# A four-layer kernel with the work of its attention half-steps timed anew and its matrix splits in uneven portions

## The chip, the cores and the metric

The kernel runs on one core of a Trainium2 chip. The metric is the device time of one execution in microseconds (us); with several executions, their median. Everything is float32 on the outside. TensorE (PE) multiplies, VectorE (DVE), ScalarE (ACT) and GpSimd (POOL) do the elementwise work, and nearly all transfers are issued by SyncE (SP) on one queue.

## The reference

The input x has 2048 rows of 640 numbers. Four residual layers follow each other: attention, Fourier mixing, attention, Fourier mixing. Each first normalizes its input by row.

```python
def _A_ref(x, wqkv, wo):
    H = 32; Dh = D // H
    W, dil = 8, 2
    qkv = (lambda x, *d: x.transpose(*d))((x @ wqkv).reshape(B, S, 3, H, Dh), 2, 0, 3, 1, 4)
...
    logits = jnp.einsum("bhsd,bhswd->bhsw", q, kg) * scale
...
    o = jnp.einsum("bhsw,bhswd->bhsd", attn, vg)
    return (lambda x, *d: x.transpose(*d))(o, 0, 2, 1, 3).reshape(B, S, D) @ wo

def _B_ref(x, dft_seq_re, dft_seq_im, dft_hid_re, dft_hid_im):
    a = jnp.einsum("bsd,ed->bse", x, dft_hid_re)
    b = jnp.einsum("bsd,ed->bse", x, dft_hid_im)
    y = jnp.einsum("ts,bse->bte", dft_seq_re, a) - jnp.einsum("ts,bse->bte", dft_seq_im, b)
    return y
```

Attention is local: each row looks at eight rows (itself and every second one before it), in 32 heads of 20 numbers.

## The kernel before

Every float32 factor is split into a high part that TensorE takes in one pass (a cast on ACT) and a low part, the rest (a subtraction on DVE or POOL). A product is then three matmuls: high times high, high times low, low times high (`PASSES`, L283). The rows are held in four chunks c of four tiles j, 128 rows each.

**An attention layer** (`layer_a`) is called twice: for layer 0 (called A0 below, `CFG['ly'][0]`) and for layer 2 (A2, `CFG['ly'][1]`). Its attention runs over 32 units u, eight to a chunk, a unit being four heads, and each unit has two halves jp, so that there are 64 steps, with some 7 steps of entry before them and a few behind them. In a step:

- DVE multiplies the queries with the keys of the window (`qk_mul`, L498); POOL adds the two halves of every product (L501); DVE sums the rest into logits (`qk_red`, L511). A pair (u, jp) listed in `whole` leaves out POOL's addition, and DVE sums twice as many numbers.
- DVE and ACT do the softmax (`soft`, L524 to L537, parts 0 to 5; `soft_exp`, L519). DVE multiplies the weights with the values (`av_mul`, L541), and POOL adds the eight products in three halvings (`av_tree`, L556 to L558).
- ACT copies a unit's queries into PSUM ahead of its first half (`q_copy`, L471).
- TensorE works beside it: `qkv_mm` (L429) makes queries, keys and values, 64 groups g of 15 matmuls, whose results ACT copies out (`qkv_evac`, L436) and SP stores to HBM, from where the windows are loaded; transposes of normalized input or of attention output (`pc_pe`, L394; high part `pc_hi`, L398; the high part subtracted in PSUM, `pc_sub`, L402; low part `pc_lo`, L417); the output projection `wo_mm` (L581), which DVE adds to the residual (`wo_add`, L217); and, in the last 18 steps, the first sequence product of the Fourier layer that follows (`z_mm`, L969), 16 slices of 15 matmuls.
- For that product the new rows are normalized: `ln_hi` on ACT, and the low part `ln_lo` (L919), which `lnv` sends to DVE (1) or POOL (0), one entry for each tile. The reciprocal root of the variance is a power on POOL (`finish`, L239), or, where `lno` of the chunk is true, a logarithm and an exponential on ACT (`var_eps`, L227). The product's other factor, a slice of the cosine matrix, is split in A0 (`c_hi` L941, `c_lo` L954) and read back from HBM already split in A2 (`c_get`, tile c0b).

The order of all this is written by hand. Each piece of work is put at a step and a phase (`at`), and in each step the phases are gone through in the order of the string `ph` (the first for steps below 48, the second for the others); the result is the order of each engine's queue, SP's too. The engines work their queues in order, and between them only data and free buffers make one wait. `gs` gives the step of each QKV group, `wo` those of the projection halves, `z` three times the step of each third of a slice (the remainder picks the phase z0, z1 or pe3), `ln` the step of the normalization, `t2` and `t3` those of the last transposes, `ym` and `ymph` the step and phase of the previous layer's last two output tiles (`ymm`, L1043), `early` the order in which A2's first tiles are transposed inside the end of the layer before, and `wqg` which weight splits of the start go to POOL.

**A Fourier layer** (`LayerB`) is a sequence product by a seven-product scheme (`pair`, L1132), three pairs of row blocks, with the second sequence product and the preparation ahead of it (`run`): cell sums of the matrix blocks (`x_whole` L1088, `x_combine` L1096 to L1098) and the splits of the hidden matrices (`load_w`, L188 to L192) are 38 items that the lists `pre` and `post` deal out over 16 slices of that product. There the order is by hand only for TensorE; a planner orders the rest.

## Time and profile before

| | us |
|---|---|
| three runs: median (lowest to highest) | 1796.12 (1793.09 to 1797.68) |
| the profiled execution, its own time | 1798.85 |
| its span, first to last instruction | 1797.1 |
| TensorE busy | 1737.8 |
| VectorE busy | 1375.7 |
| ScalarE busy | 818.1 |
| GpSimd busy | 633.3 |

How to read it: the profile comes from one execution, and its span is 1.75 us shorter than that execution's own time. GpSimd works only in the two attention layers. A matmul that waits inside a chain of matmuls still counts as busy in part, so the busy time of TensorE is an upper bound of its work. The chain of waits follows the end back from releaser to releaser; the views by stage (windows) give each engine's busy time in a stretch, and the clock granted to TensorE as a share of the full one.

### The profile page before, as it was taken

Reading aid. Unit: us, or ns where it says so; the run is one execution under the profiler, and the core shown is the slowest. Engines: PE = TensorE matmul, PEld = TensorE weight load, DVE = VectorE, ACT = ScalarE, POOL = GpSimd, SP = SyncE. Lnnn points to the kernel's source line nnn. Section 1 sums busy time; section 2 is a strip of 40 time slices with the busy share of each in tenths; the row PEclk is TensorE's granted clock in tenths of the full one; section 3 lists DMA queues with packets and bytes.
Section 4 is the critical chain, followed back from the end, with each engine's and each line's share of the span. In section 5 each row is a group of like instructions: output and inputs, shape, how many; then the busy total and the mean of one; then the engine's idle time right before and its main releaser. Section 6 shows DMA issues by size and latency. Waiting matters only on the chain.

```text
span 1797.1 us, 26504 instructions
## 1 busy us (share of the span) xinstructions
PE 1737.8 (97%) x8798; PEld 1508.5 (84%) x8798; DVE 1375.7 (77%) x2136; ACT 818.1 (46%) x1708; POOL 633.3 (35%) x591
## 2 busy tenths in 40 slices
PE   9999998989999999999999999999899999999999
PEld 6889897778788888888888899987788888888888
DVE  5899889888767767768739988888777676676673
ACT  5554544544445545445533334444434443443441
POOL 3799898960000000000008987889400000000000
PEclk9999998999999999999999999999999999999999
DMA  6786667647787887888747856687687876877861
GB/s 231 225 279 212 202 207 253 221 154 276 255 268 245 292 272 242 291 271 267 246 126 224 283 182 202 202 293 263 218 289 269 258 235 216 272 234 224 264 212 52
DMA packets 273994, 423.59 MB, mean 236 GB/s; under 512 B 22688, under 2 KB 153248, under 8 KB 273600
## 3 DMA queue, kind: packets, MB, share of 16 engines
q1 hardware_dynamic: 270656, 419.92, 71.7%
q10 hardware_dynamic: 3200, 1.97, 0.4%
q8 instruction: 70, 1.15, 0.3%
q14 instruction: 68, 0.56, 0.1%
HBM read 336.66 MB, written 85.14 MB: 235 GB/s over the span
## 4 chain that ended last, share of the span: by engine, by line
PE 67%; DVE 11%; DMA 9%; POOL 7%; ACT 3%; issue 2%; SPq 0%; ACTq 0%; DVEq 0%; POOLq 0%
PE m L429 18%; PE aux L1043 12%; PE t L1132 9%; PE m L1132 9%; PE pq L1132 5%; PE xt L1132 5%; PE aux L581 4%; DMA win<-cs_in 3%; DMA xc<-stg 2%; POOL pr L556 2%; DVE pr L498 2%; POOL pr L501 2%; DVE pr L541 2%; POOL r L919 1%; PE t L969 1%
## 5 line engine op out<-in xcount | busy, mean ns | idle before, releaser
L429 PE MATMUL m<-r,s 128*128 128x480 f32 x1920 | 438.4, 383 | 4.3 <-ACT s L297 3.2
L429 PEld LDWEIGHTS m<-r,s 128*128 128x128 f32 x1920 | 358.0, 189 | 58.6 <-ACT s L297 4.9
L1125 ACT CAST r<-win 128x512 fp32r<-128x512 f32 x251 | 153.0, 620 | 175.3 <-DVE win L1161 90.2
L239 POOL TENSOR_TENSOR stats<-stats,mhalf 128x1 f32<-128x1 f32 (+1 forms) x40 | 28.9, 723 | 567.8 <-ACT stats L233 567.8
L1043 PE MATMUL aux<-r2a,zo 128*128 128x320 f32 x768 | 226.0, 309 | 0.0
L556 POOL TENSOR_TENSOR pr<-pr 128x640 f32<-128x640 f32 x126 | 204.2, 1621 | 36.6 <-DVE pr L541 36.0
L498 DVE TENSOR_TENSOR pr<-pq,win 128x1280 f32<-128x1280 f32 x128 | 189.7, 1483 | 28.7 <-ACT pq L471 26.3
L1043 PE MATMUL aux<-pr,zo 128*128 128x320 f32 x704 | 207.8, 309 | 0.0
L1126 DVE TENSOR_TENSOR r<-win,r 128x512 fp32r<-128x512 f32 x251 | 169.4, 687 | 44.0 <-ACT r L1125 42.1
L541 DVE TENSOR_TENSOR pr<-pq,win 128x1280 f32<-128x1280 f32 x128 | 190.9, 1491 | 4.3
L501 POOL TENSOR_TENSOR pr<-pr 128x640 f32<-128x640 f32 x128 | 183.5, 1434 | 22.0 <-DVE pr L498 19.1
L1132 PE MATMUL m<-r,r 128*128 128x512 f32 x594 | 152.4, 391 | 1.2 <-ACT stg L1097 0.5
L1043 PEld LDWEIGHTS aux<-r2a,zo 128*128 128x128 f32 x768 | 144.2, 188 | 1.9
L969 PE MATMUL m<-s,r 128*128 128x512 f32 x384 | 120.8, 402 | 17.7 <-DMA s<-c0b 8.0
L1043 PEld LDWEIGHTS aux<-pr,zo 128*128 128x128 f32 x704 | 132.2, 188 | 2.0
L1132 PEld LDWEIGHTS m<-r,r 128*128 128x128 f32 x594 | 111.0, 188 | 26.0 <-DVE r L1126 1.4
L1132 PE MATMUL t<-r,r 128*128 128x512 f32 x495 | 132.5, 390 | 0.0
L436 ACT COPY stg<-m 128x480 f32<-128x480 f32 x128 | 71.1, 556 | 115.9 <-PE m L429 100.8
L969 PE MATMUL t<-s,r 128*128 128x512 f32 x384 | 118.0, 396 | 2.4 <-DVE ot L1025 2.4
L511 DVE TENSOR_REDUCE lg<-pr 128x64 f32<-128x640 f32 x128 | 104.2, 814 | 18.0 <-POOL pr L501 17.8
L557 POOL TENSOR_TENSOR pr<-pr 128x320 f32<-128x320 f32 x126 | 114.0, 905 | 9.9
L1132 PEld LDWEIGHTS t<-r,r 128*128 128x128 f32 x495 | 92.9, 188 | 19.9
(271 smaller groups left out, 3221.0 us busy)
## 6 DMA issues: line engine op xcount, KB each, us to landing
win<-cs_in SPq DMA_DIRECT2D x358, 256.0 KB, 4.4
r<-xc SPq DMA_DIRECT2D x240, 256.0 KB, 4.5
win<-kvb SPq DMA_DIRECT2D x96, 440.0 KB, 4.5
xa<-cs_in SPq DMA_DIRECT2D x124, 256.0 KB, 4.3
win<-kvb SPq DMA_DIRECT2D x64, 360.0 KB, 5.0
xc<-stg SPq DMA_DIRECT2D x40, 512.0 KB, 4.8
kvb<-stg SPq DMA_DIRECT2D x60, 320.0 KB, 4.0
xr<-xs SPq DMA_DIRECT2D x40, 320.0 KB, 3.3
```

Source lines behind the costliest of these rows:

```text
L429: nc.tensor.matmul(mt[g][:, : 3 * F], st[:, a, k], wq[q][:, b, k], start=n == 0, stop=n == 14)
L498: nc.vector.tensor_tensor(pr, q, wview(u, jp, 0, [[1, FE]]), op=ALU.mult)
L501: nc.gpsimd.tensor_tensor(pv[:, :, 0:10], pv[:, :, 0:10], pv[:, :, 10:20], op=ALU.add)
L511: nc.vector.tensor_reduce(rows(lgs[u], jp), pv.rearrange("p (a h) d -> p a h d", h=HE), axis=AX.X, op=ALU.add,)
L541: nc.vector.tensor_tensor(pr.rearrange("p j w (h d) -> p (j w) h d", d=DH), rows(lgs[u], jp).unsqueeze(3).to_broadcast([P, 2 * W, HE, DH]) ...
L556: g.tensor_tensor(pr[:, :, 0:4], pr[:, :, 0:4], pr[:, :, 4:8], op=ALU.add)
L557: g.tensor_tensor(pr[:, :, 0:2], pr[:, :, 0:2], pr[:, :, 2:4], op=ALU.add)
L969: self.last = nc.tensor.matmul(self.z[t][k], self.xn[c][:, a, j, k * P : (k + 1) * P], self.ct[s][:, b], start=s == 0 and i == 0, stop=s = ...
L1043: self.last = nc.tensor.matmul(self.ym[e][:, :320], zt[(k, a, ri)][:, j2 * P : (j2 + 1) * P], w[:, e * 320 : (e + 1) * 320], start=(k, a, ...
L1125: nc.scalar.copy(hi, raw)
L1126: nc.vector.tensor_tensor(lo, raw, hi.bitcast(F32), op=ALU.subtract)
L1132: nc.tensor.matmul(bank, w(a, kb), hl[b], start=start and (a, b) == (0, 0), stop=stop and (a, b) == (1, 0),)
```

## The change

The lists of `CFG` are set anew for both attention layers and for the two `run` stages. In A0 two halves, (u, jp) = (16, 1) and (28, 1), become `whole`; the low parts of tiles (0,0), (0,2), (0,3) and (1,1) go from POOL to DVE and those of (3,2) and (3,3) from DVE to POOL; the DVE order puts softmax part 4 ahead of `qk_red` in steps below 48 and `av_mul` ahead of part 1 in the others. In A2 the low part of (0,3) goes to DVE and that of (3,2) to POOL, the statistics of chunks 2 and 3 take the logarithm on ACT, the previous layer's two output tiles stand behind QKV groups 2 and 5 and no longer behind 3 and 4, and the transposes of chunk 2 and 3 that shared steps are spread over more steps. Some QKV groups, projection halves, thirds of slices and loads move by a step or two in both. The items of `run` are dealt out unevenly, a few ahead of a slice.

In `pair` the loading and splitting of an iteration is put into three helpers, so that it could be issued ahead; with `ahead` at [0, 0, 0] and `views` empty nothing is. The splits of an iteration now stand ahead of its products in the program's text (all three in the first loop, the first two in the others), in the same order among themselves as before. The diff, with the second and third helper and the loops that call them cut:

```diff
-CFG = {'nwin': 5,
+CFG = {'views': [],
+ 'ahead': [0, 0, 0],
+ 'nwin': 5,
  'bufs': {'xa': 2, 'qs': 1, 'stg': 2, 'xr': 1},
  'pad2': 16,
  'ot': ['ot'],
- 'wqg': [0, 0, 0, 0, 0, 0, 1, 0, 1, 0, 0, 1, 0, 1, 0, 0, 1, 0, 1, 0],
- 'run': [{'pre': [0, 0, 0, 0, 0, 0, 0, 0, 0, 0, 0, 0, 0, 0, 0, 0],
-          'post': [0, 4, 4, 4, 3, 3, 3, 3, 3, 3, 3, 3, 3, 3, 3, 3],
+ 'wqg': [0, 0, 0, 0, 0, 0, 0, 0, 1, 0, 0, 1, 0, 0, 0, 0, 1, 1, 0, 0],
+ 'run': [{'pre': [0, 0, 0, 0, 0, 0, 0, 1, 0, 0, 0, 4, 0, 0, 0, 0],
+          'post': [1, 5, 4, 2, 3, 3, 2, 6, 3, 1, 0, 3, 1, 3, 3, 3],
           'y': [[6, 6, 6, 6, 6], [13, 13, 16, 16, 16]]},
-         {'pre': [0, 0, 0, 0, 0, 0, 0, 0, 0, 0, 0, 0, 0, 0, 0, 0],
-          'post': [0, 4, 4, 4, 3, 3, 3, 3, 3, 3, 3, 3, 3, 3, 3, 3],
-          'y': [[6, 6, 6, 6, 6], [13, 13, 16, 16, 16]]}],
- 'ly': [{'gs': [-7, -6, -5, -4, -3, -2, -1, 0, 1, 1, 2, 3, 3, 4, 5, 5, 6, 7, 8, 8, 9, 11, 12, 12, 13, 14, 14, 15, 16,
-                16, 17, 18, 18, 19, 20, 21, 22, 23, 24, 25, 26, 27, 28, 29, 30, 30, 31, 32, 33, 34, 34, 35, 36, 37,
-                38, 39, 40, 41, 42, 43, 44, 45, 46, 47],
+         {'pre': [0, 0, 0, 0, 0, 6, 0, 0, 2, 0, 0, 0, 0, 0, 0, 0],
+          'post': [0, 4, 4, 5, 0, 2, 1, 1, 0, 5, 6, 0, 5, 1, 6, 0],
+          'y': [[6, 6, 6, 6, 6], [12, 13, 16, 16, 16]]}],
+ 'ly': [{'gs': [-7, -6, -5, -4, -3, -2, -1, 0, 1, 2, 2, 2, 3, 4, 5, 5, 6, 7, 8, 8, 9, 11, 12, 12, 13, 14, 14, 14, 16,
+                16, 16, 18, 18, 19, 20, 21, 22, 23, 24, 25, 25, 27, 28, 29, 30, 30, 31, 32, 33, 33, 34, 35, 36, 37,
+                39, 39, 41, 41, 42, 43, 44, 45, 46, 46],
          'tx': [4, 6, 8, 10, 16, 18, 20, 22, 30, 32, 34, 36],
-         'ord': [[0, 2, 1, 3, 4, 6, 5, 7], [0, 2, 1, 3, 4, 6, 5, 7], [0, 2, 1, 3, 4, 6, 5, 7]],
+         'ord': [[2, 0, 1, 3, 4, 6, 5, 7], [0, 2, 1, 3, 4, 6, 5, 7], [0, 2, 1, 3, 4, 6, 5, 7]],
          'out': [20, 24, 28, 32, 36, 40, 44, 46],
-         'wo': [22, 23, 26, 27, 30, 31, 34, 35, 38, 39, 42, 43, 46, 47, 48, 49],
+         'wo': [23, 23, 26, 27, 30, 30, 34, 35, 37, 38, 42, 43, 46, 47, 49, 49],
          'woph': 'pe2',
-         'ln': [40, 42, 44, 46, 52, 53, 54, 55],
+         'ln': [40, 43, 44, 46, 53, 53, 55, 54],
          'w2': [52, 53, 54, 55],
          'w3': [60, 61],
          'lnown': [4, 3],
-         'z': [149, 149, 149, 152, 152, 152, 155, 156, 157, 161, 161, 164, 170, 170, 170, 173, 173, 173, 173, 173,
-               173, 174, 176, 176, 179, 179, 179, 179, 180, 181, 185, 188, 188, 188, 191, 191, 191, 191, 194, 195,
-               199, 200],
+         'z': [149, 149, 151, 151, 151, 152, 152, 154, 155, 161, 163, 163, 170, 170, 170, 172, 173, 173, 174, 175,
+               176, 176, 177, 178, 180, 182, 182, 182, 185, 185, 185, 186, 186, 188, 191, 191, 191, 191, 194, 195,
+               198, 200],
          'early': [3, 3, 6.5, 8.7, 5, 6, 7, 8.5, 10, 11, 14, 14.1, 8],
          'ym': [-3, -2],
          'ymph': 'pe3',
-         't2': [48, 48, 48, 48, 52, 52, 52, 52],
-         't3': [58, 58, 60, 60],
-         'ph': ['peT0 dma evac hi z0 pe peL pe2 z1 fin red0 dma2 qk sA sB av0 sD red1 sE sC loE exp evacA actL evacO '
-                'actl sF av1 qc dmaw dmas misc dmac dmar pe3w pe3',
-                'peT0 dma evac hi z0 pe peL pe2 z1 fin red0 dma2 qk sA sB av0 sD red1 sE sC loE exp evacA actL evacO '
-                'actl sF av1 qc dmaw dmas misc dmac dmar pe3w pe3'],
+         't2': [48, 48, 47, 48, 52, 52, 52, 51],
+         't3': [57, 58, 60, 60],
+         'ph': ['peT0 pe dma evac hi z1 z0 peL pe2 fin red0 dma2 qk sA sB av0 sD sE red1 sC loE exp evacA actL actl '
+                'sF evacO av1 qc dmaw dmas misc dmac dmar pe3w pe3',
+                'peT0 dma hi evac z0 pe peL pe2 z1 fin red0 dma2 qk sA av0 sD sB red1 sE loE sC actL exp evacA actl '
+                'sF evacO dmac av1 qc dmas misc dmar dmaw pe3 pe3w'],
          'xst': 3,
          'xld': 4,
          'lnx': False,
          'lno': [False, False, False, False],
-         'whole': [],
-         'lnv': [0, 0, 0, 0, 0, 0, 0, 0, 0, 0, 0, 0, 1, 1, 1, 1]},
-        {'gs': [-7, -6, -5, -4, -2, 0, 0, 1, 1, 2, 3, 4, 4, 6, 6, 7, 8, 9, 10, 10, 11, 13, 14, 14, 15, 16, 17, 18, 18,
-                19, 20, 21, 22, 22, 23, 24, 25, 26, 26, 27, 28, 29, 30, 30, 31, 32, 33, 34, 34, 35, 36, 37, 38, 39,
-                40, 40, 41, 42, 42, 43, 44, 45, 46, 47],
-         'tx': [6, 8, 10, 12, 18, 20, 22, 24, 32, 34, 36, 38],
-         'ord': [[0, 2, 1, 3, 4, 6, 5, 7], [0, 2, 1, 3, 4, 6, 5, 7], [0, 2, 1, 3, 4, 6, 5, 7]],
-         'out': [20, 24, 28, 32, 36, 40, 44, 46],
-         'wo': [22, 23, 26, 27, 30, 31, 34, 35, 38, 39, 42, 43, 46, 47, 48, 49],
-         'woph': 'pe2',
-         'ln': [40, 42, 44, 46, 52, 53, 54, 55],
+         'whole': [33, 57],
+         'lnv': [1, 0, 1, 1, 0, 1, 0, 0, 0, 0, 0, 0, 1, 1, 0, 0]},
+        {'gs': [-7, -6, -5, -4, -3, -1, 0, 1, 2, 2, 3, 4, 5, 6, 6, 7, 8, 9, 10, 10, 11, 13, 14, 14, 15, 16, 16, 17,
+                17, 18, 19, 20, 21, 22, 23, 24, 25, 25, 26, 27, 29, 29, 30, 30, 31, 32, 33, 33, 34, 35, 36, 37, 38,
+                39, 40, 41, 41, 42, 42, 43, 44, 46, 46, 47],
+         'tx': [6, 8, 10, 12, 18, 20, 22, 23, 32, 34, 36, 38],
+         'ord': [[0, 2, 1, 3, 4, 6, 5, 7], [2, 0, 1, 3, 4, 6, 7, 5], [0, 2, 1, 3, 4, 6, 5, 7]],
+         'out': [20, 25, 29, 32, 36, 41, 44, 46],
+         'wo': [22, 23, 28, 28, 30, 31, 34, 35, 38, 39, 42, 43, 46, 47, 48, 49],
+         'woph': 'z1',
+         'ln': [42, 42, 44, 46, 52, 54, 55, 56],
          'w2': [52, 53, 54, 55],
          'w3': [60, 61],
          'lnown': [4, 3],
-         'z': [149, 149, 149, 152, 152, 152, 155, 155, 156, 157, 161, 164, 167, 170, 170, 170, 170, 173, 173, 173,
-               173, 174, 176, 176, 179, 179, 179, 180, 181, 185, 188, 188, 188, 191, 191, 194, 194, 194, 194, 195,
+         'z': [148, 151, 152, 152, 155, 155, 155, 157, 158, 159, 163, 164, 165, 168, 169, 170, 171, 173, 173, 173,
+               173, 175, 178, 179, 179, 180, 180, 182, 182, 182, 185, 186, 188, 188, 188, 190, 191, 194, 194, 195,
                199, 200],
-         'early': [3, 3, 6.5, 8.7, 5, 6, 7, 8.5, 10, 11, 14, 14.1, 8],
-         'ym': [-3, -2],
-         'ymph': 'pe3',
-         't2': [48, 48, 48, 48, 52, 52, 52, 52],
-         't3': [58, 58, 60, 60],
-         'ph': ['peT0 dma evac hi z0 pe peL pe2 z1 fin red0 dma2 qk sA sB av0 sD red1 sE sC loE exp evacA actL evacO '
-                'actl sF av1 qc dmaw dmas misc dmac dmar pe3w pe3',
-                'peT0 dma evac hi z0 pe peL pe2 z1 fin red0 dma2 qk sA sB av0 sD red1 sE sC loE exp evacA actL evacO '
-                'actl sF av1 qc dmaw dmas misc dmac dmar pe3w pe3'],
+         'early': [3, 5, 7.5, 8.7, 5.6, 6, 7.3, 8.8, 8.7, 10, 14, 14.1, 8],
+         'ym': [-5, -1],
+         'ymph': 'z1',
+         't2': [48, 49, 48, 48, 50, 52, 51, 52],
+         't3': [59, 58, 60, 61],
+         'ph': ['peT0 dma evac hi z0 pe peL pe2 z1 fin red0 dma2 sA qk sD sB av0 red1 sE sC loE exp evacA actL actl '
+                'sF evacO av1 dmaw dmas qc misc dmar pe3w pe3 dmac',
+                'peT0 dma hi evac z0 pe peL pe2 z1 red0 fin dma2 sA qk sB av0 sD red1 sE sC loE exp evacA actL actl '
+                'sF evacO av1 dmaw dmas qc misc dmar pe3w pe3 dmac'],
          'xst': 3,
          'xld': 4,
          'lnx': False,
-         'lno': [False, False, False, False],
+         'lno': [False, False, True, True],
          'whole': [],
-         'lnv': [1, 0, 1, 0, 0, 0, 0, 0, 1, 1, 1, 1, 1, 1, 1, 1]}]}
+         'lnv': [1, 0, 1, 1, 0, 0, 0, 0, 1, 1, 1, 1, 1, 1, 0, 1]}]}
...
+            AH = CFG["ahead"]
+
+            def ahead_a(i):
+                b22, b21, b11 = raw(t2, NP + i), raw(t1, NP + i), raw(t1, i)
+                x5, x7 = self.x_slot(5, i, ring), self.x_slot(7, i, ring)
+                c5 = split(b22)
+                c4 = split(combine(b11, b21, b11, ALU.subtract))
+                return x5, x7, c5, c4, split(combine(b22, b21, b22, ALU.add))
...
                 m5, m4, m7 = banks("m0", "m1"), banks("xt", "t0"), banks("t1", "pq")
                 for i in range(NP):
                     ends = i == 0, i == NP - 1
-                    b22, b21, b11 = raw(t2, NP + i), raw(t1, NP + i), raw(t1, i)
-                    x5, x7 = self.x_slot(5, i, ring), self.x_slot(7, i, ring)
-                    self.product(m5, x5, split(b22), *ends)
-                    c4 = split(combine(b11, b21, b11, ALU.subtract))
+                    x5, x7, c5, c4, c7 = self.ahead.pop(("a", p)) if i == 0 and ("a", p) in self.ahead else ahead_a(i)
+                    self.product(m5, x5, c5, *ends)
                     self.product(m4, self.x_plain(*k2(i), 256), c4, *ends)
-                    c7 = split(combine(b22, b21, b22, ALU.add))
                     self.product(m7, x7, c7, *ends)
+                b0 = ahead_b(0) if AH[0] else None
...
```

More of the change, by code (lines that the diff above doesn't have):

```diff
@@ L905, in __init__ @@
             self.whole = {}
+            self.ahead = {}
             self.nraw = self.nhl = self.nx = 0
@@ L1151, in pair @@
             ]
-            views = cells[0] + ["s0", "s1"]
+            views = cells[0] + ["s0", "s1"] + CFG["views"]
             def raw(t, s):
@@ L1209, in pair @@
                     ends = i == 0, i == NP - 1
-                    b11, b22, b21 = raw(t1, i), raw(t2, NP + i), raw(t1, NP + i)
-                    x2, x1 = self.x_slot(2, i, ring), self.x_slot(1, i, ring)
-                    p11 = split(b11)
+                    x2, x1, p11, p22, rest = b0 if i == 0 and b0 else ahead_b(i)
                     self.product(m2, x2, p11, *ends)
                     self.product(f1, self.x_plain(*k1(i), 512), p11, i == 0, False)
-                    p22 = split(b22)
                     self.product(f2, self.x_plain(*k2(i), 512), p22, i == 0, False)
-                    c1 = split(combine(b22, b11, b22, ALU.add))
+                    c1, p21 = rest()
                     self.product(m1, x1, c1, *ends)
-                    p21 = split(b21)
                     self.product(f1, self.x_plain(*k2(i), 512), p21, False, i == NP - 1)
+                if hooks is not None:
+                    views = cells[0] + cells[1] + CFG["views"]
+                ring = ring[NJ:]
+                d0 = ahead_c(0) if AH[1] else None
                 es = store("stg", CFG["bufs"]["stg"])
@@ L1243, in pair @@
                         tags = narrow
-                    b12, b22, b11 = raw(t2, i), raw(t2, NP + i), raw(t1, i)
-                    x6 = self.x_slot(6, i, ring)
-                    c3 = split(combine(b22, b12, b22, ALU.subtract))
+                    x6, c3, p12, rest = d0 if i == 0 and d0 else ahead_c(i)
                     self.product(m3, self.x_plain(*k1(i), 0), c3, *ends)
-                    p12 = split(b12)
                     self.product(f2, self.x_plain(*k1(i), 512), p12, False, i == NP - 1)
-                    c6 = split(combine(b11, b11, b12, ALU.add))
-                    self.product(m6, x6, c6, *ends)
+                    self.product(m6, x6, rest(), *ends)
                     if self.li == 1 and i < KEEP[p]:
```

14 lines of the change are left out of this document (11 added, 3 removed).

## The prediction

> **What bounds the kernel now.** I read the page first, then the engines by stage, then the chain of waits inside the stages that lose time.
>
> ```profile
> span 1797.1 us, 26504 instructions
> PE 1737.8 (97%) x8798; PEld 1508.5 (84%) x8798; DVE 1375.7 (77%) x2136; ACT 818.1 (46%) x1708; POOL 633.3 (35%) x591
> ```
>
> TensorE is busy for 97% of the span, so all that waits are removed can bring is some 59 us, 3%. The stages say where these lie. Columns: stretch, its length, then busy us (and instructions) of PE, weight load, DVE, ACT, POOL, then the granted clock.
>
> ```profile
> 87.30:207.50 120.20, 119.31 (x599) 105.03 (x600) 108.73 (x152) 64.75 (x168) 112.35 (x107) 0.97 0.73 235
> 207.50:278.40 70.90, 70.88 (x387) 63.78 (x385) 64.06 (x99) 33.73 (x83) 64.61 (x59) 1.00 0.71 218
> 278.40:403.20 124.80, 106.88 (x538) 91.72 (x538) 109.51 (x165) 58.37 (x141) 103.14 (x92) 0.93 0.62 203
> 403.20:483.80 80.60, 76.62 (x373) 64.56 (x374) 60.23 (x91) 35.09 (x64) 0.00 (x0) 1.00 0.76 265
> ...
> 1078.00:1178.00 100.00, 100.00 (x537) 90.28 (x536) 83.65 (x126) 45.06 (x110) 81.92 (x76) 1.00 0.66 207
> 1178.00:1295.40 117.40, 105.82 (x562) 91.99 (x560) 96.54 (x153) 50.37 (x128) 94.40 (x88) 0.97 0.75 255
> 1295.40:1373.60 78.20, 75.43 (x369) 64.28 (x370) 60.26 (x91) 33.73 (x59) 0.00 (x0) 1.00 0.79 276
> ```
>
> The middle of either attention layer (rows 1, 2 and 5) is TensorE's: it has next to no gap. The ends (steps 48 on, rows 3 and 6) are not: TensorE idles 17.9 us in A0 and 11.6 us in A2, at a lower granted clock, and waits for attention. The chain of waits of A0's end names who is late; columns are start, length, what.
>
> ```profile
> 249.22 1.53 POOL r L919
> 250.76 1.39 POOL pr L501
> ...
> 270.21 1.54 POOL r L919
> ...
> 296.31 3.72 DMA r<-x_in
> ...
> 321.35 1.53 POOL r L919
> ...
> 337.59 1.38 POOL pr L501
> 338.97 1.99 POOL pr L556
> ...
> 352.47 1.54 POOL pr L556
> ```
>
> Around the lines of POOL the chain is POOL piece after POOL piece without a gap, as the first two lines show: there POOL is the bound, though the page gives it 35%. Each low part (L919) in it lengthens A0 by its own length.
>
> **The change part by part.** *Term 1, POOL's list in A0.* Of the low parts in that chain, those at 249.22 and 270.21 are tiles (0,0) and (0,2), counted by their places, and that at 321.35 is (1,1); all go to DVE. Half (28,1), `whole` after the change, loses the addition at 337.59. That is 1.53 + 1.54 + 1.53 + 1.38 = 5.98 us off a saturated list; (0,3) and half (16,1) stand outside the chain and count nothing. DVE takes them over:
>
> ```profile
> L919 DVE TENSOR_TENSOR r<-xa,r x6: 814/1038/1177, 379.6 to 1273.6; 128x640 fp32r<-128x640 f32 x6
> L919 DVE TENSOR_TENSOR r<-r,r x4: 812/882/1470, 1230.7 to 1249.9; 128x640 fp32r<-128x640 f32 x4
> L511 DVE TENSOR_REDUCE lg<-pr x128: 805/812/824, 40.9 to 1267.2; 128x64 f32<-128x640 f32 x128
> ```
>
> A low part costs DVE 0.81 to 1.47 us, and the sum over twice as many numbers at most another 0.81, an estimate by doubling the last row. DVE's idle time covers that, 6.8 us before 278.4 and 15.3 us behind. Before 278.4, however, TensorE is full, so attention that comes 3.07 us earlier is worth only what it brings into the end; I take half, 1.5, and the later 2.91 in full: **-4.4** (ends 0 and -5.98).
>
> *Term 2, a transfer in A0.* The piece at 296.31 is a load of residual rows that SP issues ahead of the loads of windows, and DVE's next multiplication waits behind it. The change moves the first of them one step later. It is not removed: **-1.0**, nearer to 0 than to -3.7.
>
> *Term 3, POOL's list in A2.*
>
> ```profile
> 1180.37 1.52 POOL r L919
> ...
> 1192.83 4.58 DMA s<-c0b
> ...
> 1219.19 0.51 POOL stats L239
> ...
> 1225.74 0.52 POOL stats L239
> ...
> 1232.91 0.51 POOL stats L239
> ...
> 1263.09 5.11 DMA s<-c0b
> ```
>
> The first, tile (0,3), goes to DVE; it stands where TensorE's full stage ends, so half of it, 0.76. The three powers belong to chunk 2 and go to ACT, 1.54. In their place ACT has a logarithm and an exponential more for each; no row shows a logarithm, and the nearest on 128x1 is ACT's L247, below. ACT is busy for 50.4 of 117.4 us, so they hide. **-2.3** (0 to -3.1).
>
> ```profile
> L247 ACT ACTIVATE stats<-stats 128x1 f32<-128x1 f32 x28 | 8.3, 298 | 5.7 <-POOL stats L239 5.5
> L156 ACT ACT_TABLE_LOAD x1 | 1.3, 1283 | 0.7 <-PEq L1360 0.7
> ```
>
> The second row is the run's only table load. If a logarithm needed another table, eight tiles would cost two loads each, 20.5 us of ACT. [...]
>
> *Term 4, loads of split slices in A2.* Two of them stand in the chain above; all such waits of TensorE are here (us, times, longest):
>
> ```profile
> PE m L969 <- DMA s<-c0b: 8.0, 6, 2.8
> ```
>
> Slice 1 is now needed a third and two rounds of transposes later, while its load is issued in the same step; that wait, the longest, should close. The later ones move with their loads. **-2.5** (0 to -8.0).
>
> *Term 5, the entry of A2.* In order of time on TensorE:
>
> ```profile
> 908.66 0.71 PE L429 MATMUL m<-r,s 128*128 128x480 f32 x2 [1.85 <-ACT s L297]
> ...
> 910.26 3.07 PE L429 MATMUL m<-r,s 128*128 128x480 f32 x13 [0.57 <-ACT s L297]
> ```
>
> Group 3 waits 2.42 us for its transposed tile. In the chain 60 matmuls of an output tile follow, for 8.79 us:
>
> ```profile
> 913.33 8.79 PE aux L1043 x60
> ```
>
> The change puts them ahead of group 3, where they cover the wait; the other tile likewise goes behind group 5. **-2.4** (0 to -2.4).
>
> *Term 6, transposes spread over steps.* In A2 chunk 2 and 3 now have seven more steps in which the subtraction in PSUM follows its transposes with no product between, so it waits for ACT's cast, as it does here in A0:
>
> ```profile
> 302.63 0.58 PE L402 MATMUL aux<-ot,nident 128*128 128x256 f32 x1 [1.21 <-ACT s L398]
> ```
>
> That is up to 8.5 us of holes. TensorE's idle time covers those before 1262 us; from there the chain runs through TensorE, and two lie there: **+2.4** (0 to +8.5). A0 has three, inside its 17.9 us.
>
> *At nothing.*
>
> ```profile
> L534 DVE RECIPROCAL pq<-pq 128x16 f32<-128x16 f32 x64 | 16.4, 256 | 0.1
> ```
>
> DVE's new order lets an operation of this length (or two) change places with one that may wait for POOL, once a step, where the other engine's list is full anyway; if it filled a wait in each of 16 late steps, 4 us. The low parts of (3,2) and (3,3) go to POOL when it is idle, 1.5 against 0.8 us, but without DVE's queue ahead of them. The QKV groups keep TensorE's order but for exchanges; what they do to ACT's queue is a rival. `wqg` falls where DVE waits for casts. In `run`, TensorE idles 4.0 and 2.8 us around it (rows 4 and 7), the bound for uneven portions either way; the helpers of `pair` issue the same instructions in the same order.
>
> **Sum:** -4.4 - 1.0 - 2.3 - 2.5 - 2.4 + 2.4 = **-10.2 us**. The profiled execution took 1798.85 us, 2.7 above the median of the runs, and would take 1788.7; from the median of 1796.1 it is **1785.9 us**.
>
> **Rivals.** *More.* If every bound comes through and the transposes hide, 5.98 + 3.72 + 3.08 + 8.0 + 2.42 = 23.2 us go: **1773 us**. For it speaks that holes cost twice, the clock being 0.93 and 0.97 where they lie; against it, that the terms of one stage follow each other in one chain, and a second wait shows when the first is gone.
>
> *Little: DVE and POOL stand in each other's way.*
>
> ```profile
> L954 DVE TENSOR_TENSOR s<-win,s x34: 679/685/694, 395.5 to 1360.2; 128x512 fp32r<-128x512 f32 x34
> L954 DVE TENSOR_TENSOR s<-stg,s x14: 679/1018/2051, 282.4 to 376.2; 128x512 fp32r<-128x512 f32 x14
> ```
>
> The same subtraction takes 0.69 us after POOL has stopped and up to 2.05 us beside it, and POOL's L556 beside it took 1.99 us in place of 1.54 (two of A0's chain lines). A low part moved to DVE may so hold both: term 1 is nothing, term 3 keeps its 1.5, terms 4 and 6 cancel, and 1.0 + 1.5 + 2.4 = 4.9 us are left: **1791 us**, no change. [...]
>
> *Slower: attention tied closer to TensorE.* ACT's queue is in order. Some groups now share a step with the one or two before them, and their copies stand ahead of the query copy or the exponential of that step, where they stood behind:
>
> ```profile
> 118.67 6.69 PE L429 MATMUL m<-r,s 128*128 128x480 f32 x30
> ...
> 125.68 0.42 ACT L471 COPY pq<-qs 128x320 f32<-128x320 f32 x1
> 126.03 0.55 ACT L436 COPY stg<-m 128x480 f32<-128x480 f32 x1
> ```
>
> Here the copy of group 30 comes behind the query copy; after the change it comes first, at a cost of 0.9 us, and had TensorE been one group later, of 3.3 us (6.69 for two). DVE waits for query copies already:
>
> ```profile
> DVE pr L498 <- ACT pq L471: 26.3, 15, 5.0
> ```
>
> That is 26.3 us in 15 waits, and attention that falls behind in the full stage is late in the end, so that terms 1 and 3 go too and 3.5 us of gain are left. One group lost in either layer gives 1799; it decides from 1.33 groups on (3.5 + 5.4 over 6.69); two give 13.4 - 3.5: **1806 us**. Against it: DVE idles 11.5 us in the first row of stages and can catch up.
>
> **How the numbers follow.** The measurement of this kernel tells about 0.3% from no change, 1790.7 to 1801.5 us. The forecast, 1776 to 1790.7, has 0.45; more than that 0.20; no change, mostly the lock, 0.17; slower 0.18. So faster 0.65, same 0.17, slower 0.18. The range goes from 1768, all bounds and some of `run`'s 6.8 us, to 1803, most of the way to the slower rival, and leaves a tenth out on either side.
>
> **What would show it.** Term 1: the stretch from step 48 to the end of A0 shorter by some 4 us, with L919 at those places on DVE under 1.2 us. Terms 3 and 4: A2's end shorter, no L239 of chunk 2 in the chain, waits for c0b under 6 us. Term 5: no wait of L429 for L297 around 909. Wrong would be: a table load more, A0's middle longer than 120 us with DVE waiting for L471, or the time moving in the Fourier layers, to which I give nothing.

## The result, and the profile after

The change makes the kernel faster: 1785.15 us (median of four runs, 1783.94 to 1786.93), a ratio of 0.9937 to the runs of before on the same chip, 95% interval 0.9917 to 0.9958. That is 11.3 us, with an interval of 7.5 to 14.9. The first two lines that the page of after answers to those of before:

```profile
span 1785.1 us, 26486 instructions
PE 1734.6 (97%) x8798; PEld 1502.7 (84%) x8798; DVE 1381.3 (77%) x2140; ACT 821.2 (46%) x1716; POOL 625.0 (35%) x577
```

TensorE has the same 8798 matmuls and is busy 3.2 us less; POOL gave 8.3 us and 14 instructions away, DVE and ACT took some of them. The span is 12.0 us shorter. The engines by stage, after; the columns are those of the same view of before, and the last two are the busy share of the DMA engines and what they moved (GB/s):

```profile
206.20:276.60 70.40, 69.45 (x377) 62.51 (x376) 66.61 (x102) 34.15 (x83) 64.28 (x58) 1.00 0.65 206
276.60:401.90 125.30, 107.31 (x553) 90.91 (x551) 112.12 (x164) 59.22 (x143) 102.92 (x91) 0.96 0.63 210
401.90:481.30 79.40, 77.76 (x373) 65.91 (x374) 61.18 (x93) 34.87 (x64) 0.02 (x1) 0.98 0.77 270
...
907.20:971.00 63.80, 63.80 (x335) 57.33 (x334) 38.79 (x56) 19.85 (x44) 31.86 (x30) 1.00 0.58 181
...
1171.50:1283.00 111.50, 103.95 (x562) 89.41 (x560) 95.36 (x151) 53.50 (x136) 89.55 (x79) 1.00 0.78 268
```

Row 2, A0's end, was 124.80 us and is 125.30: nothing came out of it, though step 48 begins 1.8 us earlier. Row 5, A2's end, was 117.40 us and is 111.50; TensorE idles 7.6 us there in place of 11.6. Row 4 is A2's entry and first steps, in which TensorE has no gap left; the same stretch of before:

```profile
910.00:980.00 70.00, 68.23 (x360) 61.32 (x361) 40.72 (x57) 20.45 (x47) 33.58 (x31) 1.00 0.56 170
```

It took 70.0 us and takes 63.8. The ends of such windows were put at like places by eye: row 2 holds 15 matmuls more than before, row 4 has 25 fewer, so that its 6.2 us are not all gain. Further down the distances are taken from matmul to matmul; by them A2's entry, from QKV group 0 to 16, is 5.1 us shorter. So most of the gain lies in A2, in its entry and its end, and none shows in A0's attention. The chain of waits through A0's end, after, says why:

```profile
303.54 5.35 DMA win<-kvb
308.94 1.34 issue
310.31 0.90 DVE r L219 x4
...
313.34 1.41 DVE pr L543
315.31 1.93 DVE r L922
317.24 0.82 DVE r L219 x4
318.06 1.41 DVE pr L500
...
325.49 3.39 DMA stg<-cs_in
...
329.79 1.88 DVE s L957
331.67 1.41 DVE pr L500
```

Before, POOL piece after POOL piece stood here. Now DVE's own list and two kinds of transfers (windows, slices of the cosine matrix) hold the end up: from 297 to 336 us the chain has no POOL piece, from 336 to 363 us it is POOL's again. The low part that went to DVE (L922, L919 of before) is itself in the chain, at 1.93 us.

The two layers' lists and those of `run` were then tried apart, and after them their parts, each against the kernel before.

### The profile page after: what moved, and what is told of

Same layout as the page of the kernel before. It is cut to its first block, busy times and chain, and to the rows that moved or that the text cites. A ratio compares the mean times of both kernels' runs of the same rounds, so it can differ in the third digit from the quotient of the medians.

```text
span 1785.1 us, 26486 instructions
## 1 busy us (share of the span) xinstructions
PE 1734.6 (97%) x8798; PEld 1502.7 (84%) x8798; DVE 1381.3 (77%) x2140; ACT 821.2 (46%) x1716; POOL 625.0 (35%) x577
## 4 chain that ended last, share of the span: by engine, by line
PE 74%; DVE 11%; DMA 7%; ACT 3%; POOL 2%; issue 2%; SPq 0%; DVEq 0%; ACTq 0%; POOLq 0%
PE m L431 19%; PE aux L1046 14%; PE t L1135 10%; PE m L1135 10%; PE pq L1135 5%; PE xt L1135 5%; PE aux L583 5%; DMA xc<-stg 3%; DVE pr L500 2%; DVE pr L543 2%; DMA win<-cs_in 2%; PE m L972 1%; PE t L972 1%; DVE lg L513 1%; DVE s L957 1%
## 5 line engine op out<-in xcount | busy, mean ns | idle before, releaser
L241 POOL TENSOR_TENSOR stats<-stats,mhalf 128x1 f32<-128x1 f32 (+1 forms) x32 | 23.5, 735 | 474.3 <-ACT stats L235 474.3
L972 PE MATMUL m<-s,r 128*128 128x512 f32 x384 | 121.4, 403 | 10.6 <-ACT r L918 2.7
L513 DVE TENSOR_REDUCE lg<-pr 128x64 f32<-128x640 f32 (+1 forms) x128 | 104.3, 815 | 7.3 <-POOL pr L503 7.3
```

Source lines behind the costliest of these rows:

```text
L513: nc.vector.tensor_reduce(rows(lgs[u], jp), pv.rearrange("p (a h) d -> p a h d", h=HE), axis=AX.X, op=ALU.add,)
L972: self.last = nc.tensor.matmul(self.z[t][k], self.xn[c][:, a, j, k * P : (k + 1) * P], self.ct[s][:, b], start=s == 0 and i == 0, stop=s = ...
```

## The experiments

**Which lists.** Three kernels, each the kernel before with one group of lists of the change:

```diff
 # first: A0 and wqg      # second: A2              # third: run
-'ly'[0]: before          -'ly'[1]: before          -'run': before
+'ly'[0]: after           +'ly'[1]: after           +'run': after
-'wqg': before
+'wqg': after
```

> The kernel before with the lists of A0 alone set anew (its steps, phases, low parts, whole halves, and wqg). The prediction's terms 1 and 2: 5.4 us faster, about 1790.7, with A0's end (from step 48 to the last matmul of slice 15) shorter by that. Theory from the two traces: attention in A0 reaches step 63 about 1.8 us earlier, and the end gives that back, because the low part of tile (3,3) on POOL waits for DVE's cell sum: 0 to 1.5 us faster, the first matmul of the pairs at about 483 us.

> The kernel before with the lists of A2 alone set anew. The prediction's terms 3 to 6 (without term 1 and 2): 4.8 us faster, half of it at the entry. Theory from the two traces: nearly the whole gain is here, 8 to 10 us, some 3 at the entry by QKV group 8, 2 more by group 16, and 5 to 7 behind step 48.

> The kernel before with the lists pre, post and y of the two run stages alone set anew. The prediction: 0, inside plus and minus 6.8 us. Theory from the two traces: 2 to 3 us faster, all of it in the first run stage, between slice 0 of the second sequence product and the first pair; nothing in the second.

| lists | ratio to before | interval | us faster |
|---|---|---|---|
| A0 and `wqg` | 0.9983 | 0.9968 to 0.9997 | 3.1 (0.5 to 5.8) |
| A2 | 0.9941 | 0.9926 to 0.9956 | 10.6 (7.9 to 13.3) |
| `run` | 0.9987 | 0.9976 to 0.9999 | 2.3 (0.2 to 4.3) |

(The last column is one minus the ratio, times the median of before on the same chip, 1797.4 to 1798.9 us in these and the later runs.) By the prediction's terms A0 was to bring 5.4 us and A2 4.8; A2's lists alone are worth nearly the whole change. The three add up to 16.0, more than the 11.3 measured together, but the intervals allow either.

One execution places gains of 2 us badly. The distance from step 48 of A0 to the last matmul of the first half of its slices is 127.6 to 129.5 us in the ten profiled kernels with A0's lists of before, or with some low parts alone moved, and 129.0 to 130.0 in the four with the lists of after, which begin it 1.0 to 1.8 us earlier. Nothing reaches the end of A0's attention. The end of the second half comes at 474.0 to 475.8 us in these four, at 475.4 to 479.0 in the others: if A0's 3.1 us are real, they lie there, behind attention. Which list makes them wasn't tried.

**Term 1 alone.** The low parts (0,0), (0,2), (0,3), (1,1) to DVE and two halves `whole`, in the kernel before:

```diff
-         'whole': [],
-         'lnv': [0, 0, 0, 0, 0, 0, 0, 0, 0, 0, 0, 0, 1, 1, 1, 1]},
+         'whole': [33, 57],
+         'lnv': [1, 0, 1, 1, 0, 1, 0, 0, 0, 0, 0, 0, 1, 1, 1, 1]},
```

> The kernel before with term 1 alone: in A0 the low parts of (0,0), (0,2), (0,3) and (1,1) go to DVE and the halves (16,1) and (28,1) become whole. The prediction: 4.4 us faster (between 0 and 6). [...] A third theory, that POOL's list is no longer the longest once two of its pieces are gone, so that DVE or a transfer is late next: 1 to 2 us faster, with the chain of A0's end on DVE for longer.

Measured: 0.9998, interval 0.9986 to 1.0010: 0.4 us (-1.8 to 2.5), nothing that can be told from zero, and less than the 4.4 forecast. POOL was relieved, though by less than the pieces taken from it are long. A0's end by engine in this kernel:

```profile
278.40:403.20 124.80, 106.49 (x538) 90.21 (x537) 112.07 (x165) 57.81 (x140) 98.87 (x88) 0.95 0.61 202
```

POOL is at 98.87 us where it was at 103.14, DVE at 112.07 where it was at 109.51. What DVE waited for POOL from 200 to 403 us, in the kernel before (us, times, longest):

```profile
DVE lg L511 <- POOL pr L501: 8.6, 7, 2.8
```

and in this kernel, and then what POOL waited for DVE, in before and in this kernel:

```profile
DVE lg L511 <- POOL pr L501: 1.9, 2, 1.3
```

```profile
POOL pr L556 <- DVE pr L541: 6.2, 10, 1.7
```

```profile
POOL pr L556 <- DVE pr L541: 12.1, 14, 2.2
```

The wait changed sides: 6.7 us less on DVE, 5.9 us more on POOL. From 278 to 300 us the chains of both kernels run through DVE and loads. Where before has POOL pieces alone, from 301 to 365 us, this kernel's runs through DVE and loads from 312 to 352 us, as in after:

```profile
316.13 1.02 DVE r L919
318.37 3.85 DMA stg<-cs_in
...
326.19 1.50 DVE pr L498
...
330.55 2.01 DVE s L954
332.58 4.25 DMA stg<-cs_in
...
344.78 3.13 DVE s L954 x2
347.91 1.41 DVE pr L498
```

Both kernels come to the same point: in before the chain has `DVE pr L498` at 366.03 us, here at 366.18. These are two lists, each feeding the other, with a queue of loads beside them. What DVE no longer waits, 6.7 us, it pays in work: over both stretches from 207.5 to 403.2 us it is busy 5.75 us more.

Did DVE and POOL stand in each other's way (rival *Little*)? In part they did. The two stretches together, in before and in this kernel:

```profile
sum 195.70, PE 177.75 PEld 155.50 DVE 173.57 ACT 92.09 POOL 167.74; mean PE 88.88 PEld 77.75 DVE 86.78 ACT 46.05 POOL 83.87
```

```profile
sum 195.70, PE 177.37 PEld 154.07 DVE 179.32 ACT 91.78 POOL 163.04; mean PE 88.69 PEld 77.04 DVE 89.66 ACT 45.89 POOL 81.52
```

Five of the six pieces that changed engine lie in them; half (16,1) lies ahead. By its own length DVE's part of this comes to 4.0 us: four low parts at the shortest of the row below (0.82; two of its five were DVE's before, and the fourth that moved is in a row of another form, at 1.11), and for the half 1.48 us for the doubled sum in place of 0.81.

```profile
L919 DVE TENSOR_TENSOR r<-xa,r x5: 815/978/1686, 246.1 to 383.3; 128x640 fp32r<-128x640 f32 x5
```

DVE's 5.75 are 1.8 more than that, 1.1 of it in the four low parts themselves. POOL gave away 7.7 us, four low parts (6.3) and an addition (1.4), and is busy only 4.7 us less, so what it kept takes 3.0 us longer. That is not scatter: POOL's operations on 128x640 with output `pr` take 1.547 to 1.558 us on the average of these stretches in the nine kernels that leave the four low parts on POOL, and 1.577 to 1.585 in the five that do not. Each of the four meets a POOL operation, and one or both run long: at 246.07 and 276.13 us DVE needs its 0.81 and POOL's L556 beside it 2.08 and 2.07 in place of the usual 1.57; at 265.62 they need 1.69 and 2.16; at 316.05 DVE needs 1.11 and POOL's L501 2.02 in place of some 1.4. Over both engines 1.8 and 3.0 us are lost, 4.8 in all, of the size that would make the term nothing. How the zero divides between this and the two lists that feed each other isn't shown; no run has the one without the other.

**The parts of A2.** Four kernels, each the kernel before with one part of A2's lists: the two output tiles; the logarithms on ACT; thirds of slices with the last transposes; the phase strings.

```diff
-         'ym': [-3, -2],                            # first
-         'ymph': 'pe3',
+         'ym': [-5, -1],
+         'ymph': 'z1',
-         'lno': [False, False, False, False],       # second
+         'lno': [False, False, True, True],
-         'z': [149, 149, 149, 152, 152, 152, ...],  # third
-         't2': [48, 48, 48, 48, 52, 52, 52, 52],
-         't3': [58, 58, 60, 60],
+         'z': [148, 151, 152, 152, 155, 155, ...],
+         't2': [48, 49, 48, 48, 50, 52, 51, 52],
+         't3': [59, 58, 60, 61],
-         'ph': A2's strings of before               # fourth
+         'ph': A2's strings of after
```

> The kernel before with A2's two output tiles alone as after the change (ym [-5, -1], phase z1): they cover group 3's wait. By term 5 of the prediction 2.4 us faster (0.9987), with the wait of L429 for L297 gone around 909 us. By what the traces of before, of after and of all A2 lists together show, the entry of A2 up to group 8 is 3.4 to 4 us shorter: 3.4 us faster (0.998), nothing of it lost behind, since the middle of A2 is TensorE's. Rival, the terms do not add up alone: the cover moves the other early work, the entry is shorter by under 1 us, 0.9995 or above.

> The kernel before with the logarithm and the exponential on ACT in place of POOL's power for chunks 2 and 3 of A2, alone. By term 3 of the prediction three powers of 0.51 us leave a saturated list of POOL: 1.5 us faster (0.9992). By the second theory, that the end of A2 waits for DVE and transfers once POOL gives way, as the end of A0 did with four low parts fewer on POOL (0.9998): nothing, 0.9997 to 1.0003. Against both, if the logarithm needs a table of its own: some 20 us slower (1.011), with 16 more table loads in the trace. Doubling is not at stake: the trace of after has the new instructions at about 0.3 us each.

> The kernel before with the thirds of the slices (z) and the last transposes (t2, t3) of A2 alone as after the change. By terms 4 and 6 of the prediction the waits for c0b fall from 8.0 to under 6 us (2.5 gained) and the subtractions wait for ACT's cast (2.4 lost): no change, 0.9999. Theory from the traces: the waits for c0b nearly all go (1.3 us are left after the change) and the transposes' waits, 8.2 us after the change, lie where TensorE has time: 4 to 6 us faster (0.997 to 0.998), all of it behind step 48 of A2. Rival: the end is DVE's and the loads only follow; the waits go elsewhere and the time is unchanged within 0.5 us.

> The kernel before with A2's two phase strings alone as after the change: softmax part 0 ahead of the multiplication with the keys and part 5 ahead of the additions on DVE, copies of attention output later on ACT, stores behind. By the prediction nothing (a wait filled in each of 16 late steps would be 4 us at most). By the second theory, in which DVE sets the end of A2: 2 to 4 us faster (0.998 to 0.999), behind step 48. Rival: the new order only serves the other lists, and alone it is slower by 1 us or more, since attention output comes later to the transposes.

| part | ratio | interval | us faster |
|---|---|---|---|
| output tiles | 0.9966 | 0.9955 to 0.9977 | 6.1 (4.1 to 8.1) |
| logarithms | 0.9994 | 0.9982 to 1.0005 | 1.1 (-0.9 to 3.2) |
| thirds, transposes | 0.9998 | 0.9988 to 1.0008 | 0.4 (-1.4 to 2.2) |
| phases | 0.9996 | 0.9987 to 1.0005 | 0.7 (-0.9 to 2.3) |

The output tiles are the largest single part. What TensorE waited for in A2's entry (880 to 980 us), before:

```profile
PE m L429 <- ACT s L297: 2.7, 3, 1.9
PE xt L394 <- ACT xa L256: 1.5, 1, 1.5
```

and with the tiles moved:

```profile
PE xt L394 <- ACT xa L256: 1.5, 1, 1.5
```

The first row is gone, and from the first matmul of group 0 to that of group 8 the trace has 53.5 us in place of 57.0: 3.5 us. The trace of before is a cheap case of this wait, though. Seven of the profiled kernels keep it, and take 56.7 to 60.7 us from group 0 to 8. In the two longest, term 1 alone (59.6) and the phases alone (60.7), TensorE is granted half its clock for 6.8 us behind the hole, from about 907 to 914 us; in the other five, and in the seven kernels that have cover for the wait, it has the full clock there. 880 to 940 us in before and with the phases:

```profile
880.00:940.00 60.00, 57.18 (x331) 52.33 (x331) 27.27 (x49) 27.40 (x60) 2.45 (x3) 1.00 0.47 144
```

```profile
880.00:940.00 60.00, 56.43 (x314) 51.51 (x313) 24.41 (x45) 25.13 (x55) 2.11 (x3) 0.94 0.43 129
```

Against the mean of the seven, 58.0, the tiles are worth 4.5 us here, an estimate that lies inside the interval of 4.1 to 8.1.

No table was loaded for the logarithms: this is the only row of its kind in that kernel, and the new instruction is short.

```profile
L156 ACT ACT_TABLE_LOAD x1 | 1.3, 1283 | 0.7 <-PEq L1360 0.7
```

```profile
L230 ACT ACTIVATE stats<-stats,eps 128x1 f32<-128x1 f32 x8 | 2.4, 295 | 0.3
L231 ACT ACTIVATE stats<-stats 128x1 f32<-128x1 f32 x8 | 1.6, 203 | 0.3
```

With eight logarithms and eight exponentials more on ACT, the whole run has one load of 1.28 us, as the run of before has. Alone, though, none of the last three parts can be told from nothing. With thirds and transposes alone the waits of TensorE for c0b (1160 to 1300 us) are down from 8.0 us to 0.5, those of the subtractions for ACT's cast are up from none to 4.4, and the time is the same within 2 us.

**The parts together, and in their final place.** The four parts at once; the lists of A2 that none of the four has (QKV groups, transposes, projections, `early`, normalization, two low parts) alone; the kernel after with the output tiles set back; and the kernel after with A0's last two low parts set back on DVE.

```diff
 # the first two on the kernel before, the others on the kernel after
+         'ym', 'ymph', 'lno', 'z', 't2', 't3', 'ph': as after          # four parts
+         'gs', 'tx', 'ord', 'out', 'wo', 'woph', 'ln', 'early', 'lnv': as after   # the rest of A2
-         'ym': [-5, -1],                            # after without the tiles
-         'ymph': 'z1',
+         'ym': [-3, -2],
+         'ymph': 'pe3',
-         'lnv': [1, 0, 1, 1, 0, 1, 0, 0, 0, 0, 0, 0, 1, 1, 0, 0]},     # after, A0's last low parts on DVE
+         'lnv': [1, 0, 1, 1, 0, 1, 0, 0, 0, 0, 0, 0, 1, 1, 1, 1]},
```

> The kernel before with A2's output tiles, logarithms, thirds with transposes, and phases together, each of which ran alone. If they add up: 6.1 + 1.1 + 0.4 + 0.7 = 8.3 us faster (0.9954). Rival, the gains of A2's end need each other: over 9.5 us faster (0.9947 or below), close to all of A2's lists. Second rival, the alone-measured ones are only noise and the output tiles are all: 6.1 (0.9966).

> The kernel before with all of A2's lists that none of the runs so far set alone: QKV groups, input transposes, output transposes and projections, order of the first tiles (early), normalization steps and the two low parts; without the output tiles, the logarithm, thirds and phases. All of A2 is worth 10.6 us and the output tiles 6.1. Theory, the parts add up: logarithm, thirds and phases gave 1.1 + 0.4 + 0.7, so 2.3 us remain for these lists, 0.9987, in the first steps (the wait of L394 for L256, 1.5 us, gone) and behind step 48. Rival: the rest of the gain is of lists that work only together, and this alone is 0 or slower (1.000 or above).

> The kernel after with A2's two output tiles back behind groups 3 and 4, nothing else. If covering group 3's wait is the change's largest part in its final place too, the waits of L431 for L299 come back with 2.4 us or more and it is 4 to 6 us slower than after (1.0025 to 1.0035), about 1790. Rival: the new order of the first tiles has covered that wait by other work, and it is less than 1.5 us slower.

> The kernel after with the low parts of tiles (3,2) and (3,3) of A0 back on DVE, nothing else. After the change the last of them took POOL 2.30 us beside DVE's cell sum of 1.22, against DVE's 0.82 before; from the normalization on ACT to the next product it is 2.5 us instead of 1.9, and TensorE is granted 0.88 of its clock around it instead of 1.00. Theory: the prediction's reason for costing this at nothing (POOL is idle) was wrong, and the version is 1 to 2 us faster than after (0.9992), about 1783.5. Rival: DVE's queue ahead of it costs as much, the same time within 0.5 us.

| kernel | ratio to before | interval | us faster than before |
|---|---|---|---|
| four parts of A2 | 0.9949 | 0.9934 to 0.9964 | 9.2 (6.5 to 11.9) |
| the rest of A2 | 0.9977 | 0.9965 to 0.9989 | 4.1 (2.0 to 6.3) |
| after, tiles set back | 0.9945 | 0.9931 to 0.9959 | 9.9 (7.4 to 12.4) |
| after, low parts set back | 0.9927 | 0.9908 to 0.9946 | 13.1 (9.7 to 16.5) |

The rest of A2 was not nothing, and setting the tiles back in the kernel after costs 1.4 us and not 4 to 6 (a difference that the intervals do not tell from zero). Distances in the traces lead both back to the entry; in us, from group to group by their first matmuls, and from step 48 to the end of the first half of the slices:

| kernel | A2, group 0 to 8 | 8 to 16 | A2's end |
|---|---|---|---|
| before | 57.0 | 29.0 | 120.1 |
| not changed there (others) | 56.9 to 59.6 | 29.0 | 117.8 to 119.8 |
| output tiles | 53.5 | 29.0 | 119.6 |
| the rest of A2 | 55.1 | 27.3 | 119.1 |
| after, tiles set back | 54.9 | 27.3 | 114.8 |
| all of A2 | 53.6 | 27.3 | 114.2 |
| after | 53.7 | 27.3 | 114.5 |
| logarithms; thirds; phases | 57.9; 56.7; 60.7 | 29.0 | 117.3; 118.1; 116.9 |
| four parts | 54.6 | 29.0 | 114.1 |

**The entry** has one wait and two covers for it. Against before's trace the tiles take 3.5 us out (2.4 in the kernel with the four parts), and the rest of A2 1.9, of which the new order of the first tiles (`early`, with the groups' steps) is the part that bears on the entry, though it wasn't tried alone; both together take out 3.3 to 3.4. With the tiles set back in the kernel after, this is all of the wait that returns (880 to 980 us):

```profile
PE m L431 <- ACT s L299: 1.0, 1, 1.0
```

So the tiles have 6.1 us on the kernel before and little on the kernel after. The other 1.7 us of the entry, from group 8 to 16, are the wait of L394 for L256, and only the rest of A2 takes it away.

**A2's end** is 4 to 5 us shorter in the kernels that have logarithms, thirds and phases together, 114.1 to 115.3 us (the last with A0's low parts set back), than in those that have none of them (117.8 to 120.1); with one alone it is 116.9 to 118.1. Each alone looks like 1 to 3 us there, at the edge of the scatter; only together do they stand out of it. By the ratios the three together are worth 3.1 us, 9.2 less the tiles' 6.1, and 9.2 us for the four against 8.3 for the sum of the four alone is what parts that add up would give. What TensorE waited for there, 1160 to 1300 us, in the kernel with the four parts:

```profile
PE aux L402 <- ACT ot L398: 2.0, 2, 1.6
...
PE aux L402 <- ACT s L398: 1.3, 3, 0.6
PE m L969 <- DMA s<-c0b: 1.3, 1, 1.3
```

The loads' waits are down from 8.0 us to 1.3. Those of the subtractions for ACT's cast, none before, are 4.4 with two smaller rows, all ahead of 1250 us. In after, with the same 4.4, the chain of waits runs through TensorE from 1182 to 1212 us and takes four of the holes in, 1.6 us (three there and one at 1247); from 1212 us to 1262 it runs mostly through DVE and ACT, so that the others lie beside it:

```profile
1225.94 1.50 DVE pr L500
1227.79 1.49 DVE pr L543
1229.48 1.47 DVE r L922
1230.95 1.41 DVE pr L500
```

In the kernel before the chain was POOL's from 1212 to 1235 us, and three powers (L239) stood in it; in after no power (L241 there) does.

**The last low parts of A0** were put to POOL. In the kernel after the last of them is slow, and TensorE waits for it; the timeline around its place:

```profile
399.62 2.30 POOL L922 TENSOR_TENSOR r<-win,r 128x640 fp32r<-128x640 f32 x1 [1.36 <-ACT r L934]
```

and with it back on DVE:

```profile
399.59 1.22 DVE L1091 TENSOR_TENSOR s<-r 128x1024 f32<-128x1024 f32 x1
400.73 0.82 DVE L922 TENSOR_TENSOR r<-win,r 128x640 fp32r<-128x640 f32 x1
```

On DVE it waits for the cell sum and is through at 401.55, 1.7 us after ACT's normalization; on POOL that is 2.4 us. The ratio of this version to before, 0.9927, is better than that of after, 0.9937, by 0.0010, but the intervals overlap almost wholly. It has the lowest ratio of all, and is not shown to beat after. The lower clock didn't go away either: from 396 to 410 us TensorE is granted 0.88 with the low part on DVE too, as in after; in before it is 1.00.

## Why the prediction was right, and where it was not

It forecast 1785.9 us and 1785.15 was measured. The place of the gain was wrong: A0 was to bring 5.4 us of the 10.2 (terms 1 and 2) and A2 4.8 (terms 3 to 6); A2 brought 10.6, and A0's attention nothing that reaches its end. Two errors of about 5 us cancelled: that the sum came out is luck, while the terms of A2's entry and end name the right places.

- **Term 1, -4.4: measured 0.4 us of gain (-1.8 to 2.5), not to be told from 0.** The step that failed is "Each low part (L919) in it lengthens A0 by its own length", from pieces in a row in the chain. A chain shows who is late, and not how late the next one is. DVE's busy 109.5 of 124.8 us stood in the row that I quoted. Its waiting for POOL fell by 6.7 us, its busy time rose by 5.75, and POOL's waiting for DVE rose by 5.9. *Little* had the right size for this term, and operations that run long beside each other are in the trace: 4.8 us on both engines, against the 5.98 that the term counted on; how much of the zero is theirs stays open. What the sentence on the chances calls the lock is this rival; no run shows a lock, only these longer times. Only one moved low part passed the 1.2 us that were named as a limit in that kernel (1.69), since the larger share of the 4.8 us, 3.0, fell on POOL.
- **Term 2, -1.0:** the load of `r<-x_in` is not among the chain's pieces in A0's end after the change, windows and cosine slices are; its end is no shorter, so the term is 0 as far as it can be seen.
- **Term 3, -2.3, and term 4, -2.5:** right in what they said would go. The powers left the chain, and the c0b waits fell by 6.7 us, far more than the one wait that I took out of 8.0. What closing them is worth was not seen apart from term 6: with thirds and transposes alone 7.5 us of these waits go and 4.4 us of the others come, for 0.4 us (-1.4 to 2.2); -2.5 and +2.4 come to the same. Of what share of A2's end each is the cause can't be told, since alone they are 1.1 and, with term 6, 0.4 us. Term 3 counts no table load for the logarithms, which no row of before could show; the runs with them have the one load of 1.28 us that before has.
- **Term 5, -2.4: mis-sized.** The cover works as described and alone is worth 6.1 us (4.1 to 8.1); against before's trace 3.5. I bounded it by the two waits ahead of group 3 and left out a third, 0.30 ahead of group 2, what matmuls lose around a wait (three gaps from matmul to matmul of 2.23, 0.84 and 0.61 us are gone), and the half clock that follows the hole in two of the seven kernels that keep it, for 6.8 us. The other 1.7 us, the wait of L394 for L256, I had not seen; the rest of A2, with the groups and `early`, costed at nothing, took it away.
- **Term 6, +2.4: mis-sized.** The waits came, 4.4 us, and 1.6 of them stand in after's chain, ahead of 1250 us and not behind 1262 as I had it; a cost of their own can't be told from the ratios.
- **At nothing:** the phases of A2, DVE's order of the softmax among them, are 0.7 us alone (-0.9 to 2.3); what they add to the shorter end together with logarithms and thirds wasn't tried apart. The low parts (3,2) and (3,3) in A0 were said to run on an idle POOL in 1.5 us; the last took 2.30, and cost some tenths at A0's end. `run` brought 2.3 us (0.2 to 4.3), so a little time did move in the Fourier layers, to which I gave nothing; where in them a single trace doesn't say: the first pair stage takes 397.1 to 401.4 us in ten kernels that are the same there. The helpers of `pair` change nothing: with the lists of before, the changed program has the same instructions in the same order on every engine.
- **Slower** did not come: DVE's waits that end with a query copy are about as long as they were, in two rows now:

```profile
DVE pr L500 <- ACT pq L473: 18.9, 11, 3.6
...
DVE lg L528 <- ACT pq L473: 6.1, 4, 2.9
```

That is 25.0 us in 15 waits; the row of before was 26.3 us in 15.

What was seen in A2's traces, terms 3 to 6 and what was costed at nothing: 5.1 at the entry and 4 to 6 at the end, 9 to 11, against 10.6 measured for A2's lists. (In the rival *More* the 3.08 should read 3.06, 1.52 + 1.54; the total stays at 23.2 by rounding.)

## What to carry to other kernels

Where two engines feed each other and a chain of waits runs along one of them, look at how much the other idles in waiting for it, and what else stands ready to be late, before counting relief of the first as gain: here 6 us off POOL were worth 0, because DVE and the loads were as late, and because work moved between these two engines ran 4.8 us longer on both together. A wait of the full engine (TensorE in A2's entry) is the opposite case: work moved into it is gained in full, but once only, whichever of two edits covers it. And changes that each look like nothing can shorten one stretch by 4 to 5 us together (3.1 by the ratios), so a list is to be judged by stage distances of several runs, not by its own ratio.

## What the runs showed of the hardware that was not expected

The granted clock after a short hole differed from execution to execution with the instructions unchanged (0.94, 0.89 and 1.00 below), and the clock records show what it went with. Three kernels that are the same from 970 to 1000 us, each with one wait of TensorE for ACT's cast, of 2.5 us in before, 3.1 with A2's thirds moved (the changes lie behind), and 3.1 with the output tiles moved; the rows of that stretch in this order:

```profile
970.00:1000.00 30.00, 27.47 (x129) 23.60 (x128) 29.01 (x41) 12.52 (x29) 28.48 (x27) 0.94 0.79 246
```

```profile
970.00:1000.00 30.00, 26.88 (x119) 22.93 (x118) 29.03 (x39) 11.12 (x27) 28.65 (x27) 0.89 0.82 265
```

```profile
970.00:1000.00 30.00, 26.88 (x131) 23.19 (x130) 28.79 (x40) 10.44 (x24) 28.61 (x27) 1.00 0.86 272
```

With the same wait of 3.1 us the clock is 0.89 in one and 1.00 in the other, and from group 16 to 32 they take 63.3 and 60.6 us. So this hole of 3 us cost itself and, in one execution of the two, up to 2.7 us more; that is the size of most single terms here. In the clock records of all 14 traces TensorE has the full clock or half of it, and every stretch at half clock inside a run is one, two or three steps of 3.41 us (in before 6.83, 10.24, 6.83 and three times 3.41 us), on a grid that lies differently in each execution: a step begins 3.37 us behind the start of the span in before, 2.11 us in after. Counted over 7170 such steps at full clock: where TensorE idled less than 1.66 us of a step, the next was never at half clock; where it idled over 1.88 us, it always was (60 of 60); in between, in 10 of 31. The hole of 3.1 us falls on one step with 2.0 us and on the next with 1.1 in the first of the two kernels, and with 1.8 and 1.3 in the second, whose clock stays full. So in these runs a hole under 1.66 us that stood alone cost only itself, and one of 3 us cost more or not by where the grid lay. The same made the two long entries of A2: the holes there put 1.85 and 1.83 us into one step.
